# AdaLN linear-attention block: first scale block in two column halves, broadcast no-ops, later w_mod halves, half of wo on the ACT queue

## Chip, cores and metric

One core of a Trainium2 chip. The metric is device time of one execution in microseconds, the median of three runs. The profile is of one execution, taken by the hardware profiler; its span is a little shorter than the measured time.

## What is computed

Inputs are x (2048 x 1024), the projection weights wqkv and wo, the feed-forward weights w_gate, w_up and w_down, a condition c (1 x 1024) and w_mod (1024 x 6144), all bf16.

```python
mod = silu(c) @ w_mod                  # six rows of 1024: sa, ca, ga, sb, cb, gb
h = layernorm(x) * (1 + ca) + sa
q, k, v = split(h @ wqkv)              # 32 heads of 32
pq, pk = phi(q), phi(k)                # phi(t) = t+1 if t>0 else exp(t), plus 1e-6
kv = sum over tokens of pk * v ; z = sum of pk
x = x + ga * ((pq @ kv) / (pq . z + 1e-6)) @ wo
h = layernorm(x) * (1 + cb) + sb
x = x + gb * ((silu(h @ w_gate) * (h @ w_up)) @ w_down)
```

## The kernel before

Tokens are worked in four blocks of 512 (`sc` = 0 to 3), each in four tiles of 128 (`t`). A block of k or v is eight groups (`k_groups`: tile t and column half nb), each of eight matmuls over the contraction chunks cc, 128x512 outputs in one PSUM bank. Four such banks (pool `pa`, `acc_a`) rotate; four more are in pool `pb` (`acc_b`). A group's bank is free again when ACT has copied it (v, line 309) or when ACT's exp (line 273) and two DVE instructions (lines 274 and 276) have turned it into phi.

**Head.** Before block 0 can start, the scale row ca is needed: silu(c) times 1024 columns of w_mod. `wca` is loaded in eight row chunks of 1024 columns, then `wv` in eight, then `wsa` and `wk`, all on the SP queue but for the first chunk. For each chunk j, `mod_rows` multiplies it into rows in PSUM (four 32-row pieces), and one matmul with one output column makes the first scale column ahead of the others (`first`). `mod_turn` turns the rows into columns. The block is normalised, transposed on TensorE (`pe_transpose_tile`), copied to `hT`, and scaled into `hs` (`scale_to`); V of block 0 runs on `hs`. The rows of sa come later. `keep_warm` issues matmuls on a zeroed tile `sel`, whose results nobody reads. `sc_row`, silu(c) in all 128 partitions, comes from eight matmuls and two ACT copies.

**Blocks.** For sc > 0: K groups 0 and 1, then kv of the block before (`kv_phase`), K groups 2 to 7, V; then statistics and transposes (`ln1`) of the next block, laid into the same stretch. `mod_load` loads 1024 columns of w_mod transposed, as two tiles; `mod_step` is one DVE instruction (line 396) that multiplies a tile's 128x1024 rows by `sc_row` and sums them into one column. The steps are spread over K and V (`K_STEPS`, `V_STEPS`); those in V wait for a flag `one` that POOL writes behind the statistics' work. `hold_back` writes one element of a new tile, so that its load does not start before a given point. At sc = 2, `wo` is loaded in eight pieces on the SP queue; later its rows are multiplied by ga.

**Fold.** While q of blocks 1 and 2 runs, kv is multiplied into wo: `fold_wo(h, nb)` runs 16 matmuls of 32 rows by 32 columns, four row groups g by four column groups i, into four banks, and copies them back into `wo` (line 611). It is called four times, each time between q groups.

**What sets the order.** Each engine runs its instructions in the order in which they stand. In the head that order is the one written (`in_order`). Elsewhere a scheduler lays out the instructions of DVE, ACT and POOL by dependencies and its own estimates; matmuls stay in the order of the text. Buffers come from rotating pools; `k8` has 19 large tiles.

Of the kernel before, what the change touches and what calls it, by code (L numbers as in the profile page):

```python
# [21 lines left out]
def kernel(  # L22
# [13 lines left out]
    nc = tc.nc  # L36
# [77 lines left out]
    c_sb = const.tile([DC, P], BF16, name="c_sb")  # L114

# [8 lines left out]
    for st in range(2):  # L124
        load_x(st, nc.sync)
# [3 lines left out]
    wca = [big("wme", [4, D]) for _ in range(2)]  # L129
# [6 lines left out]
    for j in range(DC):  # L136
        load_block(wca, wm_v, j, D, nc.scalar if j == 0 else nc.sync)
    for cc in range(DC):
        load_block(wv, wqkv_v, cc, 2 * D)
        if cc in (1, 4):  # L140
            load_x(2 + cc // 4, nc.sync)
# [26 lines left out]
    sc_row = const.tile([P, D], BF16, name="sc_row")  # L168
# [11 lines left out]
    sel = const.tile([P, HPC, P], BF16, name="sel")  # L180
# [17 lines left out]
    def bn(src, mv_out):  # L198
        stats = small.tile([P, NNB, nc.vector.BN_STATS_DIM], F32, name="stats")
        for i in range(NNB):  # L200
            nc.vector.bn_stats(out=stats[:, i, :], in_=src[:, i * NB:(i + 1) * NB])  # L201
        nc.vector.bn_aggr(out=mv_out, in_=stats[:])

    def normalise(dst, src, mean, rstd):
        nc.vector.tensor_scalar(out=dst, in0=src, scalar1=mean, scalar2=rstd, op0=ALU.subtract, op1=ALU.mult)

    def normalise_act(dst, src, mv, rstd):
        nmr = small.tile([P, 1], F32, name="nmr")
        last_nmr[0] = nc.gpsimd.tensor_scalar(out=nmr[:], in0=mv[:, 0, 0:1], scalar1=rstd[:, 0:1], scalar2=-1.0,  # L209
                                op0=ALU.mult, op1=ALU.mult)  # L210
        nc.scalar.activation(out=dst, in_=src, func=ACT.Identity, bias=nmr[:], scale=rstd[:, 0:1])  # L211
# [5 lines left out]
    def pe_transpose_tile(hT, xn, t):  # L217
        tp = acc_b("tp", (DC, P), BF16)
        for cc in range(DC):
            transpose(tp[:, cc, :], xn[:, cc * P:(cc + 1) * P])  # L220
        nc.vector.tensor_copy(out=hT[:, :, t * P:(t + 1) * P], in_=tp[:])
# [3 lines left out]
    def ln1_stats(sc, t):  # L225
        x_sb = x_tiles.pop(sc * STC + t)
        mv = small.tile([P, STC, 2], F32, name="mv")
        bn(x_sb, mv[:, 0, :])
        rstd = rstd_of(mv, 1)
        return sc, t, x_sb, mv, rstd  # L230

    def ln1_norm(sc, t, x_sb, mv, rstd, dve=False):
        xn = k2.tile([P, D], BF16, name="xn", bufs=4)
        if dve:
            normalise(xn[:], x_sb[:], mv[:, 0, 0:1], rstd[:, 0:1])
        else:
            normalise_act(xn[:], x_sb[:], mv, rstd)
        if sc > 0:
            last_load[0] = nc.sync.dma_start_transpose(hTs[sc][:, :, t * P:(t + 1) * P], xn[:])
        return xn  # L240
# [14 lines left out]
    def mod_rows(q, lo, hi, first=None):  # L255
        for j in range(lo, hi):
            if first is not None:
                mm(first, lhsT=wca[j // 4][:, j % 4, 0:P], rhs=scT[:, j:j + 1], start=False, stop=j == DC - 1)
            row_matvec(mod_ps[:, q * MW:(q + 1) * MW], sc32[:, j, :], (wsa, wca)[q][j // 4][:, j % 4, :],
                       q == 0 and j == 0, j == DC - 1)  # L260
# [4 lines left out]
    def scale_to(hs, hT, cc, lo, hi):  # L265
        nc.vector.tensor_scalar(out=hs[:, cc, lo:hi], in0=hT[:, cc, lo:hi], scalar1=ca0T[:, cc:cc + 1], scalar2=None,
                                op0=ALU.mult)

# [105 lines left out]
    def mod_load(q, cols, held=False):  # L374
        ts = [big("wmt", [DC // 2, D]) for _ in range(2)]
        if held:
            hold_back(ts)
        for h, t in enumerate(ts):
            lo = q * D + h * NB
            last = nc.sync.dma_start_transpose(t[:], w_mod[:, lo:lo + NB])  # L380
            mod_steps.extend((t[:, i, :], cols[:, 4 * h + i:4 * h + i + 1]) for i in range(DC // 2))
        return last
# [71 lines left out]
    nc.vector.memset(sel[:], 0.0)  # L454

    def keep_warm(acc, n):
        for _ in range(n):
            mm(acc[:], lhsT=sel[:, 0, :], rhs=sel[:], start=True, stop=True)

    def keep_warm_f32(acc, n):  # L460
        zeros = sel[:].rearrange("p h n -> p (h n)").bitcast(F32)
        for _ in range(n):
            mm(acc[:, 0:zeros.shape[1]], lhsT=zeros[:, 0:P], rhs=zeros, start=True, stop=True)

    accs = [acc_a() for _ in range(4)]
    spare = accs[3]
    keep_warm_f32(spare, 3)
    keep_warm(spare, 1)
# [5 lines left out]
    with in_order(nc.vector, nc.scalar, nc.gpsimd):  # L474
        mod_ps = acc_b("mod_ps")
        mm(mod_ps[:, 0:DC], lhsT=c_sb[:], rhs=ident[0:DC, 0:DC], start=True, stop=True)
        for g in range(4):
            mm(mod_ps[g * DH:(g + 1) * DH, MW:2 * MW], lhsT=ident[:, 0:DH], rhs=base_t[:, 0:MW], start=True, stop=False)
        nc.scalar.activation(out=scT[:], in_=mod_ps[:, 0:DC], func=ACT.Silu)
        xn0 = ln1_norm(*ln1_stats(0, 0))  # L480
        st1 = ln1_stats(0, 1)
        nc.vector.tensor_copy(out=sc32[:], in_=scT[:].unsqueeze(2).to_broadcast([P, DC, DH]))
        xn1 = ln1_norm(*st1, dve=True)
        keep_warm_f32(spare, 1)
        for h in range(2):
            for j in range(DC // 2):
                mm(accs[h][:, j * P:(j + 1) * P], lhsT=scT[:, 4 * h + j:4 * h + j + 1].to_broadcast([P, P]), rhs=ident[:],
                   start=True, stop=True)
            nc.scalar.copy(out=sc_row[:, h * NB:(h + 1) * NB], in_=accs[h][:])
        keep_warm(spare, 3)  # L490
        first = accs[2][:, 0:1]
        mm(first, lhsT=ident[:], rhs=base_t[:, 0:1], start=True, stop=False)
        mod_rows(1, 0, 3, first)
        pe_transpose_tile(hT, xn0, 0)
        pe_transpose_tile(hT, xn1, 1)
        mod_rows(1, 3, DC, first)
        keep_warm(spare, 1)
        nc.vector.tensor_scalar(out=hs[:, 0, 0:H], in0=hT[:, 0, 0:H], scalar1=first, scalar2=None, op0=ALU.mult)
        mod_turn(DC, 2 * DC)
        for cc in range(1, 4):  # L500
            scale_to(hs, hT, cc, 0, H)
        xn2 = ln1_norm(*ln1_stats(0, 2))
        for cc in range(4, DC):
            scale_to(hs, hT, cc, 0, H)
        st3 = ln1_stats(0, 3)
        gs = k_groups[0:4]
        v_mms(hs, gs, accs, 0, 6)
        pe_transpose_tile(hT, xn2, 2)
        for cc in range(DC):
            scale_to(hs, hT, cc, H, H + P)  # L510
        xn3 = ln1_norm(*st3)
        v_mms(hs, gs, accs, 6, DC)
        gs2, accs2 = k_groups[4:6], [acc_b("acc") for _ in range(2)]
        v_mms(hs, gs2[0:1], accs2[0:1])
        v_evac(0, gs, accs)
        pe_transpose_tile(hT, xn3, 3)
        for cc in range(DC):
            scale_to(hs, hT, cc, H + P, SCW)
        v_mms(hs, gs2[1:2], accs2[1:2])
        mod_rows(0, 0, DC)  # L520
        mod_turn(0, DC)
        nc.vector.tensor_copy(out=sca[:], in_=scr[:, :, :, 0])
        v_evac(0, gs2, accs2)
        for g in k_groups[6:8]:
            acc = acc_a()
            v_mms(hs, [g], [acc])
            v_evac(0, [g], [acc])
        modulate_all(hT, ca1T, saT)
# [4 lines left out]
    for h in range(2):  # L533
        with tc.issue_after(last_load[0].ins):
            nc.sync.dma_start(out=wq[h][:], in_=wqkv_v[:, 4 * h:4 * h + 4, 0:D])
# [5 lines left out]
    for sc in range(NSC):  # L541
        if sc > 0:
            k_phase(sc, 0, 2)
            kv_phase(sc - 1)
            k_phase(sc, 2, 3)
            if sc == 1:
                mod_load(3, sbT, True)
                mod_step(1)
            k_phase(sc, 3, 4)
            if sc == 2:  # L550
                wo = [big("wo", [4, D]) for _ in range(2)]
                hold_back(wo)
                for h in range(2):
                    for g in range(4):
                        with tc.issue_after(last_load[0].ins):
                            last_load[0] = nc.sync.dma_start(out=wo[h][g * DH:(g + 1) * DH, :, :], in_=wo_v[h, g])
            if sc == 3:
                mod_load(4, cbT, True)
            k_phase(sc, 4, 8)
        if sc == 0:  # L560
            k_phase(0, 0, 8)
# [24 lines left out]
        if sc == 0:  # L586
            with tc.issue_after(last_load[0].ins):
                last_load[0] = mod_load(2, gaT)

    q_phase(1, 0, 1, 2)  # L590
    q_phase(1, 1, 2)
# [10 lines left out]
    def fold_wo(h, nb):  # L602
        ns = slice(nb * NB, (nb + 1) * NB)
        ps = [acc_b("wf") for _ in range(4)]
        for i in range(HPC):
            for g in range(4):
                rs = slice(g * DH, (g + 1) * DH)
                mm(ps[g][i * DH:(i + 1) * DH, :], lhsT=KVT[rs, h, i * DH:(i + 1) * DH], rhs=wo[h][rs, i, ns],
                   start=True, stop=True)
        for g in range(4):  # L610
            (nc.scalar.copy if g % 2 == 0 else nc.vector.tensor_copy)(out=wo[h][:, g, ns], in_=ps[g][:])

    q_phase(1, 2, 5)
# [5 lines left out]
    den_sum(0, acc_a())  # L619
    fold_wo(0, 0)  # L620
    den_spread(0)
    q_phase(1, 6, 8)
    fold_wo(0, 1)
    q_phase(2, 0, 2)
    fold_wo(1, 0)
    q_phase(2, 2, 4)
    fold_wo(1, 1)
# [3 lines left out]
    def wo_tile(st):  # L631
# [10 lines left out]
        for nb in range(NNB):  # L642
            ns = slice(nb * NB, (nb + 1) * NB)
            a_ps = acc_b("a_ps")
            for hg in range(HG):
                mm(a_ps[:], lhsT=pq[:, hg, t * P:(t + 1) * P], rhs=wo[hg // 4][:, hg % 4, ns],
# [145 lines left out]
```

## Time and profile before

| | |
|---|---|
| Measured time, median of 3 | 830.9 us (830.61 to 830.96) |
| Profiled span | 828.4 us |
| DVE, ACT, POOL busy | 42%, 20%, 8% of the span |
| DMA, mean rate over the span | 156 GB/s |
| DMA, mean rate over the first 30 us | 359 GB/s |

How to read it: a row of the timeline has the start and the length in us, the engine, the source line, the operation, what is written and read, the shapes, and how many instructions are merged in the row. All matmuls stand at line 98, so they are told apart by their tiles: `acc<-wv,hs` is V of block 0, `acc<-wv,hT` V of a later block, `acc<-wk,hT` is K, `kvp` is kv, `wf` the fold, `acc<-hT,wq` is q. A 128x512 matmul is shown with 379 ns, but in a stream one starts every 0.216 us, since matmuls overlap; start times are what counts. About one matmul record in fifty is missing, which looks like a gap of one matmul. In the slices of the page (40 of 20.7 us each) DMA moves most in the first two:

```profile
DMA  9968444139995836456342262753405529610011
GB/s 347 301 167 187 124 112 102 41 96 320 368 246 196 251 110 181 150 168 195 103 158 96 62 222 88 254 187 110 145 0 182 149 65 358 217 47 1 19 58 51
```

### The profile page before, as it was taken

How to read it: one execution, taken by the hardware profiler on the slowest of the kernel's cores; microseconds unless marked ns; L12 is line 12 of the kernel's file. 1: busy time of each engine (PE TensorE's matmuls, PEld its weight loads, DVE VectorE, ACT ScalarE, POOL GpSimd, SP SyncE). 2: the span in 40 equal slices, each digit the busy share in tenths (PEclk: the TensorE clock that was granted, in tenths of full speed). 3: DMA queues.
4: the chain of work that ended last, by engine and by line, in shares of the span. 5: the costliest groups of instructions: out<-in, count | busy, mean ns of one | idle time of the engine just before them, and what ended most of it. 6: DMA issues, size and time to landing. Idle time of an engine off the chain costs nothing.

```text
span 828.4 us, 11209 instructions
## 1 busy us (share of the span) xinstructions
PE 818.2 (99%) x4531; PEld 379.1 (46%) x4609; DVE 348.7 (42%) x680; ACT 168.1 (20%) x253; POOL 64.0 (8%) x165
## 2 busy tenths in 40 slices
PE   8999999999999999999999999999999999999998
PEld 4444444444444444444444444444444444444444
DVE  6868778886353344422222354222224432222222
ACT  3535343434111101101111010111111101111000
POOL 2101020120222002000000010000001100000000
PEclk9999999999999999999999999999999999999999
DMA  9968444139995836456342262753405529610011
GB/s 347 301 167 187 124 112 102 41 96 320 368 246 196 251 110 181 150 168 195 103 158 96 62 222 88 254 187 110 145 0 182 149 65 358 217 47 1 19 58 51
DMA packets 142212, 129.07 MB, mean 156 GB/s; under 512 B 58768, under 2 KB 120720, under 8 KB 141648
## 3 DMA queue, kind: packets, MB, share of 16 engines
q1 hardware_dynamic: 138208, 115.10, 46.3%
q0 software_dynamic: 3792, 12.98, 5.0%
q8 instruction: 36, 0.59, 0.3%
q10 hardware_dynamic: 160, 0.26, 0.1%
q14 instruction: 16, 0.13, 0.0%
HBM read 101.98 MB, written 12.72 MB: 138 GB/s over the span
## 4 chain that ended last, share of the span: by engine, by line
PE 97%; DMA 2%; issue 1%; DVE 0%; ACTq 0%; SPq 0%
PE acc L98 89%; PE a_ps L98 7%; DMA wv<-in_A_wqkv_dram 1%; PE kvp L98 1%; DMA wme<-in_w_mod_dram 0%; PE wf L98 0%; PE den L98 0%; PE mod_ps L98 0%; PE vb L98 0%; ACTq L126 0%; PE tp L101 0%; SPq L134 0%; DVE e L708 0%; DVE ob L711 0%
## 5 line engine op out<-in xcount | busy, mean ns | idle before, releaser
L98 PE MATMUL acc<-h2T,wgu 128*128 128x512 bf16 x1755 | 385.6, 379 | 1.9
L98 PEld LDWEIGHTS <-wgu 128*128 128x128 bf16 x1792 | 175.3, 98 | 211.3
L687 DVE TENSOR_TENSOR gu<-acc,e 128x512 bf16<-128x512 f32 x112 | 77.5, 692 | 289.9 <-PE acc L98 278.8
L98 PE MATMUL acc<-wd,gu 128*128 128x512 bf16 (+2 forms) x908 | 195.2, 372 | 0.9
L686 ACT ACTIVATE e<-acc 128x512 f32<-128x512 f32 x112 | 66.9, 597 | 374.8 <-PE acc L98 363.4
L98 PEld LDWEIGHTS <-gu 128*128 128x128 bf16 x924 | 89.3, 98 | 104.5
L708 DVE TENSOR_TENSOR e<-acc,gb_bc 128x512 f32<-128x512 f32 (+2 forms) x33 | 22.3, 675 | 131.7 <-PE acc L98 122.8
L98 PEld LDWEIGHTS <-hT 128*128 128x128 bf16 x448 | 43.6, 98 | 52.3
L98 PE MATMUL a_ps<-wo,pq 128*128 128x512 bf16 x250 | 56.9, 379 | 0.3
L98 PE MATMUL acc<-hT,wq 128*128 128x512 bf16 x250 | 55.9, 379 | 0.6 <-issue 0.5
L98 PE MATMUL acc<-wk,hT 128*128 128x512 bf16 x252 | 55.9, 379 | 0.4 <-issue 0.3
L273 ACT ACTIVATE eb<-acc 128x512 bf16<-128x512 f32 x64 | 37.6, 594 | 61.7 <-PE acc L98 57.3
L211 ACT ACTIVATE xn<-x,nmr,rstd 128x1024 bf16<-128x1024 f32 x16 | 19.8, 1240 | 126.2 <-POOL nmr L209 125.4
L98 PE MATMUL acc<-wv,hT 128*128 128x512 bf16 x186 | 41.6, 379 | 0.3
L98 PEld LDWEIGHTS <-pq 128*128 128x128 bf16 x256 | 25.1, 98 | 30.2
L655 POOL DMA_DIRECT2D x_scratch<-x x16 | 9.8, 615 | 373.5 <-DVE x L648 373.4
L98 PEld LDWEIGHTS <-wq 128*128 128x128 bf16 x256 | 24.6, 98 | 29.9 <-issue 1.1
L274 DVE TENSOR_SCALAR eb<-eb 128x512 bf16<-128x512 bf16 x64 | 18.3, 290 | 26.0 <-ACT eb L273 26.0
L648 DVE TENSOR_TENSOR x<-a_ps,x_sb 128x512 f32<-128x512 f32 x32 | 22.1, 691 | 8.6 <-PE a_ps L98 7.9
L195 POOL TENSOR_TENSOR rstd<-veps,neg_half 128x1 f32<-128x1 f32 x32 | 18.0, 561 | 99.5 <-DVE veps L193 87.0
L201 DVE BATCH_NORM_STATS2 stats<-x_sb 128x6 f32<-128x512 bf16 x32 | 20.9, 674 | 4.4 <-DMA x_sb<-in_A_x_dram 4.3
L711 DVE TENSOR_TENSOR ob<-e,x1r 128x512 bf16<-128x512 f32 (+2 forms) x33 | 22.3, 675 | 1.0
(99 smaller groups left out, 320.6 us busy)
## 6 DMA issues: line engine op xcount, KB each, us to landing
wgu<-in_B_w_gate_dram SPq DMA_DIRECT2D x28, 1024.0 KB, 6.4
wgu<-in_B_w_up_dram SPq DMA_DIRECT2D x28, 1024.0 KB, 7.9
x_sb<-in_A_x_dram SPq DMA_DIRECT2D x32, 256.0 KB, 5.3
x_scratch<-x POOLq DMA_DIRECT2D x16, 512.0 KB, 3.1
x1r<-x_scratch SPq DMA_DIRECT2D x31, 256.0 KB, 2.9
wd<-in_B_w_down_dram SPq DMA_DIRECT2D x7, 1024.0 KB, 6.7
rbc<-rden_scratch POOLq DMA_DIRECT2D x16, 256.0 KB, 8.1
out_dram<-ob SPq DMA_DIRECT2D x31, 128.0 KB, 1.7
```

The costliest lines, as they stand in the source:

```text
L98: return tc.keep_in_program_order(nc.tensor.matmul(out, lhsT=lhsT, rhs=rhs, start=start, stop=stop))
L195: nc.gpsimd.tensor_tensor(out=rstd[:, 0:n], in0=veps[:, 0:n], in1=neg_half[:].to_broadcast([P, n]), op=ALU.pow)
L201: nc.vector.bn_stats(out=stats[:, i, :], in_=src[:, i * NB:(i + 1) * NB])
L211: nc.scalar.activation(out=dst, in_=src, func=ACT.Identity, bias=nmr[:], scale=rstd[:, 0:1])
L273: nc.scalar.activation(out=e[:], in_=acc, func=ACT.Exp)
L274: nc.vector.tensor_scalar(out=e[:], in0=e[:], scalar1=1.0, scalar2=PHI_EPS, op0=ALU.min, op1=ALU.add)
L648: nc.vector.tensor_tensor(out=x1[:, ns], in0=a_ps[:], in1=x_t[:, ns], op=ALU.add)
L655: nc.gpsimd.dma_start(out=x1_dram[st * P:(st + 1) * P, :], in_=x1[:])
L686: nc.scalar.activation(out=sg[:], in_=ps[0][:], func=ACT.Silu)
L687: gm = nc.vector.tensor_tensor(out=guT[sc][f // GPT][:, f % GPT, :], in0=ps[1][:], in1=sg[:], op=ALU.mult)
L708: nc.vector.tensor_tensor(out=yt, in0=y_ps, in1=gb_bc[:, ns], op=ALU.mult)
L711: nc.vector.tensor_tensor(out=ob, in0=yt, in1=x1r, op=ALU.add)
```

## The change

It has four parts.

- **Head in two column halves.** Only the first 512 columns of ca are loaded at first, in four pieces of two row chunks, and made into four scale columns directly, by matmuls with one output column (`ca_cols`); V of block 0 starts with the contraction chunks 0 to 3, of which two row tiles stand already transposed in PSUM and are scaled from there. The other 512 columns follow behind half of wv, as rows (`ca_rows`). Six instead of four V groups run on the first half. K of block 0 takes its first two groups as a pair. This is meant to start V with less loaded.
- **No-ops from a broadcast column.** `keep_warm` uses the one-column constant `neg_half`, broadcast, instead of the zeroed tile, which goes; some no-ops are shorter and placed elsewhere. `sc_row` is now computed on one partition and spread through DRAM.
- **Later loads.** The transposed loads of w_mod come as halves, each about half a block later. kv of the block before comes after one K group instead of two. Two of the four pieces of each half of `wo` are loaded on the ACT queue.
- **Fold in three.** The fold's 16 units (h, nb, g), each four matmuls, go in lots of 5, 6 and 5 instead of four lots of 4, over banks of both pools, and are copied into new tiles `wof`.

```diff
-    for j in range(DC):
-        load_block(wca, wm_v, j, D, nc.scalar if j == 0 else nc.sync)
-    for cc in range(DC):
+    load_ca(0, nc.scalar)
+    nc.scalar.dma_start(out=sc_row[0:1, :], in_=c)
+    for cc in range(4):
         load_block(wv, wqkv_v, cc, 2 * D)
-        if cc in (1, 4):
-            load_x(2 + cc // 4, nc.sync)
+    load_ca(1, nc.sync)
+    load_x(3, nc.sync)
+    for cc in range(4, DC):
+        load_block(wv, wqkv_v, cc, 2 * D)
...
+    def keep_warm(*widths):
+        for n in widths:
+            mm(accs[3][:, 0:n], lhsT=neg_half[:].to_broadcast([P, P]), rhs=neg_half[:].to_broadcast([P, n]), start=True, stop=True)
...
+        def ca_cols(k):
+            for i in range(4):
+                for j in (2 * k, 2 * k + 1):
+                    mm(cols[i], lhsT=wca[0][:, j, i * P:(i + 1) * P], rhs=scT[:, j:j + 1], start=False,
+                       stop=j == DC - 1 and i in (0, 3))
...
+        v_mms(hs, gs, accs, 0, 1)
+        turn_half(xn1, 1, 1)
...
+        v_mms(hs, gs, accs, 3, 4)
+        ca_rows()
+        mod_turn(DC + 4, 2 * DC)
...
+        v_mms(hs, gs2, accs2, 0, 4)
...
+        v_mms(hs, gs, accs, 4, DC)
+        v_evac(0, gs, accs)
+        v_mms(hs, gs2[0:1], accs2[0:1], 4, DC)
...
+        v_mms(hs, gs3[0:1], accs3[0:1])
+        mod_rows(lambda j: wsa[j // 4][:, j % 4, :], 0, DC)
...
+    nc.gpsimd.dma_start(out=sc_dram[:], in_=sc_row[0:1, :])
+    with tc.issue_after(wq_load.ins):
+        nc.sync.dma_start(out=sc_row[:], in_=sc_dram[:].to_broadcast([P, D]))
...
-            k_phase(sc, 0, 2)
+            k_phase(sc, 0, 1)
             kv_phase(sc - 1)
-            k_phase(sc, 2, 3)
+            k_phase(sc, 1, 3)
             if sc == 1:
-                mod_load(3, sbT, True)
+                mod_load(2, gaT, (1,), True)
+                mod_load(3, sbT, (0,), True)
                 mod_step(1)
             k_phase(sc, 3, 4)
             if sc == 2:
+                last_load[0] = mod_load(3, sbT, (1,), True)
                 wo = [big("wo", [4, D]) for _ in range(2)]
                 hold_back(wo)
+                behind = last_load[0].ins
                 for h in range(2):
-                    for g in range(4):
-                        with tc.issue_after(last_load[0].ins):
+                    for g in range(2):
+                        nc.scalar.dma_start(out=wo[h][(2 + g) * DH:(3 + g) * DH, :, :], in_=wo_v[h, 2 + g])
+                        with tc.issue_after(behind):
                             last_load[0] = nc.sync.dma_start(out=wo[h][g * DH:(g + 1) * DH, :, :], in_=wo_v[h, g])
...
-                last_load[0] = mod_load(2, gaT)
+                last_load[0] = mod_load(2, gaT, (0,))
...
+    wof = [big("wof", [4, D]) for _ in range(2)]
+    fold_units = [(h, nb, g) for h in range(2) for nb in range(NNB) for g in range(4)]
+
+    def fold_wo(accs):
+        units = [(fold_units.pop(0), acc) for acc in accs]
         for i in range(HPC):
-            for g in range(4):
+            for (h, nb, g), acc in units:
                 rs = slice(g * DH, (g + 1) * DH)
-                mm(ps[g][i * DH:(i + 1) * DH, :], lhsT=KVT[rs, h, i * DH:(i + 1) * DH], rhs=wo[h][rs, i, ns],
-                   start=True, stop=True)
+                mm(acc[i * DH:(i + 1) * DH, :], lhsT=KVT[rs, h, i * DH:(i + 1) * DH],
+                   rhs=wo[h][rs, i, nb * NB:(nb + 1) * NB], start=True, stop=True)
...
-    den_sum(0, acc_a())
-    fold_wo(0, 0)
+    den_sum(0)
+    fold_wo([acc_b("wf") for _ in range(3)] + [acc_a() for _ in range(2)])
     den_spread(0)
     q_phase(1, 6, 8)
-    fold_wo(0, 1)
-    q_phase(2, 0, 2)
-    fold_wo(1, 0)
-    q_phase(2, 2, 4)
-    fold_wo(1, 1)
+    q_phase(2, 0, 1)
+    fold_wo([acc_b("wf") for _ in range(4)] + [acc_a() for _ in range(2)])
+    q_phase(2, 1, 4)
+    fold_wo([acc_b("wf") for _ in range(4)] + [acc_a()])
```

## The prediction

> **What bounds the kernel now.** I read the page's shares first, then the chain of waits, then three stages of the timeline. The page:
>
> ```profile
> PE 818.2 (99%) x4531; PEld 379.1 (46%) x4609; DVE 348.7 (42%) x680; ACT 168.1 (20%) x253; POOL 64.0 (8%) x165
> PE 97%; DMA 2%; issue 1%; DVE 0%; ACTq 0%; SPq 0%
> ```
>
> TensorE is busy for 818.2 of 828.4 us, and 97% of the chain that ended last is PE. So only what shortens or stretches PE's own sequence counts. The table of PE's waits holds 1.2, 0.8, 0.7 and 0.5 us, and all but part of the 0.8 us of issue lies ahead of 12 us. The chain over the first 30 us shows what the head waits for:
>
> ```profile
> 5.52 5.48 DMA wv<-in_A_wqkv_dram
> ...
> 11.02 6.37 DMA wv<-in_A_wqkv_dram
> ...
> 17.43 3.61 PE acc L98 x16
> ```
>
> The first V matmul waits for the wv block that lands at 11.00, then for one at 17.39; from there PE runs without a break, and K starts at 27.60 (timeline). The head is bound by arrivals, the rest by PE. The stage that decides my forecast is not the head but the end of K in block 2 (sc=2), on DVE:
>
> ```profile
> 95.81 0.67 DVE L276 SCALAR_TENSOR_TENSOR pk<-acc,eb 128x512 bf16<-128x512 f32 x1
> 96.40 1.21 DVE L396 SCALAR_TENSOR_TENSOR wmt<-wmt,sc_row 128x1024 bf16<-128x1024 bf16 x1
> ...
> 98.42 0.67 DVE L276 SCALAR_TENSOR_TENSOR pk<-acc,eb 128x512 bf16<-128x512 f32 x1
> ...
> 99.87 0.67 DVE L276 SCALAR_TENSOR_TENSOR pk<-acc,eb 128x512 bf16<-128x512 f32 x1
> ...
> 103.09 0.67 DVE L276 SCALAR_TENSOR_TENSOR pk<-acc,eb 128x512 bf16<-128x512 f32 x1
> ...
> 104.71 0.15 DVE L193 TENSOR_SCALAR veps<-mv 128x1 f32<-128x1 f32 x1
> ...
> 106.03 1.28 DVE L396 SCALAR_TENSOR_TENSOR wmt<-wmt,one,sc_row 128x1024 bf16<-128x1024 bf16 x1 [0.83 <-POOL one L391]
> ```
>
> The four pk lines are the evacuations of K groups 4, 5, 6 and 7. Each frees one of the four PSUM banks of pool pa. They stand between the LayerNorm statistics of the next block, and all of them come ahead of the four modulation steps that start at 106.03.
>
> **What the Trainium skill says.** (1) "TensorE: Matmul & The Clock Gate", section "Architectural detail": matmuls keep program order and ACT and DVE are strict FIFO. The trace agrees: every DVE row above starts at or after the one before it, so an instruction put ahead delays all behind it. (2) Same page, Part 1: about 3.4 us of idleness halves the PE clock, and about 3.4 us of sustained work brings it back. No PE gap after 12 us is long enough to test the first half here; at the start, 128-column transposes run 16 in 1.07 us at 8.02, 0.056 us apart, which is the page's warm figure. (3) Same page, Part 3: matmuls on different 32x32 tiles of the array overlap. The trace agrees: 16 fold matmuls take 0.43 us. (4) "DMA: Bandwidth & Descriptors", "Issuing engines are not separate DMA queues": a second issuing queue saves only sequencer time. So half of wo on the ACT queue gains nothing in itself.
>
> **The change part by part.**
>
> Head. Transfers of 256 KB land 0.67 us apart when the queue is full (8 wk issues, each released by a landing, take 5.05 us from 18.57: (5.05-0.33)/7). Before, wv's first block is the 11th block (2 x, 8 wme), at 11.00. After, it is the 8th (3 x, 4 wme half-pieces), near 9.0. Their rows are 1 KB instead of 2 KB; on the page 1 MB of wgu (1 KB rows) lands in 6.4 us and 1 MB of wd (2 KB rows) in 6.7, so I charge nothing. Column sums, scale and rows then go on: V starts near 9.5 instead of 11.13. The next limit is the second half of the scale columns, the 15th block, at 11.00+4x0.67 = 13.7; its last rows take 0.2. From 13.9 PE still has 48 V matmuls at 0.216 (16 take 3.61-0.16, the last one's tail), 8 transposes (0.45) and the 32 rows of saT (1.06 at 23.15): 10.4+0.45+1.06 gives 25.8 for the start of K, against 27.60. A floor: the last wk block lands near 28.7 (last issue 23.29, 5.4 to landing), and the new pair of K groups needs it for its last two matmuls, so it ends at 29.2 at the earliest, against 31.05. I take -1.5 us: 1.8 less 0.3 for short waits on xn3 and on the first K evacuation. Bounds -1.9 and 0.
> The no-op matmuls from neg_half, the sc_row round trip through DRAM (needed first near 61 us, loaded behind wq near 37) and the half-tile copies on ACT cost nothing: they lie in PE's wait for DMA or in ACT's 80% idle time.
>
> Later w_mod halves and K/kv order. The steps are as many as before (1, 4, 3, 4, 4, 6, 2); each half lands at least one stage ahead of its first step. kv one K group earlier moves 128 matmuls and adds none: 0.
>
> Fold of wo. Before, four folds of 16 matmuls:
>
> ```profile
> 158.32 0.81 PE L98 MATMUL acc<-hT,wq 128*128 128x512 bf16 x3
> 159.06 0.43 PE L98 MATMUL wf<-wo,kvs 32*32 32x512 bf16 x16
> 159.43 0.82 PE L98 MATMUL acc<-hT,wq 128*128 128x512 bf16 x3
> ```
>
> The third q matmul starts at 158.32+2x0.216 = 158.75, so from the last q matmul to the next one, at 159.43, is 0.67 us; less the 0.216 that q streams anyway, a fold costs 0.45, four cost 1.82. All 16 use different tiles of the array. After, there are three folds of 5, 6 and 5 units; the fifth unit repeats a row group, so its matmul meets a tile still in use and, in FIFO order, holds up all that follow. Repeats on the same tiles do serialise: 32 saT rows of 256 columns on four tiles take 1.06 us, 8 rounds of 0.11. So a fold takes 5 streams of 0.216 in place of one: 0.45+4x0.216 = 1.31, three cost 3.94. That is +2.1 us; bounds -0.45 (one fold less, all overlapping) and +2.1.
>
> DVE order in block 2. The new order of instructions, in the changed kernel's line numbers, is:
>
> ```
> L287 pk<-acc  (K group 4)      <- V group 0 waits for this
> L407 step; the other 6 statistics, 4 aggregates, 4 veps
> L416, L418                     ga turned
> L407 x4 steps, waiting for `one` (POOL)
> L285, L287 pk<-acc (K group 5) <- V group 1 waits for this
> L285 x2, L287 x2   (K groups 6, 7)
> ```
>
> The ACT order is five exponentials, the four wo transfers, three exponentials. The banks rotate, so V group 1's first matmul waits for K group 5's evacuation, now behind the four steps. With before's durations: as before until 97.54; then the statistics without the three evacuations. These took 3x0.8, and 0.34 of idleness goes too, so the last veps ends near 102.1 instead of 104.86. `one` came 1.2 later (106.03), so the steps start at 103.3; four of 1.2 end at 108.1; the evacuation (0.2+0.69 and a gap) ends at 109.1. V starts at 99.18, so PE wants V group 1 at 99.18+1.73 = 100.9. **PE stands still for 8.2 us**, which nothing hides, since PE is the bound. The steps' durations are measured, so the bounds are narrow: 7.5 and 8.8. The stall is over twice the skill's 3.4 us, so V resumes at half clock. Cold for 3.4 us costs 1.7, for 6.8 us 3.4; a window in which half the work is enough would cost 0.8. I take 2.1.
>
> Sum: 830.9-1.5+2.1+8.2+2.1 = **841.8 us**.
>
> **Rivals.**
> A, the stall does not come, since the evacuations are reached early or V finds another bank: head and fold remain, 830.9-1.5+2.1 = 831.5. For it: PE never waits for DVE there now. Against: the order is fixed in the program and DVE is serial.
> B, faster: as A, and the fifth fold unit overlaps, 830.9-1.5-0.45 = 829.0. For it: three folds have fewer transitions than four. Against: the 8 rounds of the saT rows.
> C, the stall and nothing gained: the narrow matmuls do not keep the clock up, V's first part runs cold and the head's gain is gone, and the clock takes its full 6.8 us after the stall: 830.9+0+2.1+8.2+3.4 = 844.6.
>
> **How the numbers follow.** Main case 0.78, A 0.08, B 0.06, C 0.08. The main case spans, with its terms' ends not all at once, 838.5 to 843.5; the range goes up to C and down to 838.5, and A and B (0.14) are left out. Faster by over 0.2% is B: 0.06; within 0.2% is A: 0.08; slower 0.86.
>
> **What would show it.** Right: PE gap of about 8 us after the first eight V matmuls of block 2, ended by DVE pk L287; V matmuls after it 0.43 apart for some us; 20, 24 and 20 fold matmuls over 1.1 us each; K starting near 26. Wrong: no PE wait for DVE near 100 us, folds of 0.4 us, or V no earlier than 11.

## The result, and the profile after

| | before | after |
|---|---|---|
| Measured time, median of 4 executions each | 830.75 us | 840.6 us |
| Ratio, 95% interval | | 1.0121, 1.0106 to 1.0137 |
| Profiled span | 828.4 us | 839.7 us |
| V of block 2, first matmul to K of block 3 | 13.8 us | 24.8 us |

The change makes the kernel 1.2% slower. The page of the kernel after, busy time and granted TensorE clock:

```profile
PE 825.9 (98%) x4629; PEld 381.0 (45%) x4629; DVE 346.0 (41%) x684; ACT 174.0 (21%) x261; POOL 65.1 (8%) x167
PEclk9999979999999999999999999999999999999999
```

The busy times of the two pages can't be set against each other directly: the page before lacks some matmul records (4531 matmuls beside 4609 weight loads), this one lacks none. What stands out is one slice of 21 us (the sixth, from 105 us) with a granted clock under 0.8. The longest of PE's waits in the kernel after (total, times, longest, in us; all others are under 1 us):

```profile
PE acc L98 <- DVE pk L287: 8.4, 1, 8.4
```

It is a wait for an evacuation (line 287), which the kernel before did not have. The timeline of DVE in that stretch, K group 4's evacuation first:

```profile
96.09 0.67 DVE L287 SCALAR_TENSOR_TENSOR pk<-acc,eb 128x512 bf16<-128x512 f32 x1
...
102.09 0.15 DVE L200 TENSOR_SCALAR veps<-mv 128x1 f32<-128x1 f32 x1
...
103.86 1.28 DVE L407 SCALAR_TENSOR_TENSOR wmt<-wmt,one,sc_row 128x1024 bf16<-128x1024 bf16 x1 [1.26 <-POOL one L402]
...
107.48 1.28 DVE L407 SCALAR_TENSOR_TENSOR wmt<-wmt,one,sc_row 128x1024 bf16<-128x1024 bf16 x1
...
109.01 0.69 DVE L287 SCALAR_TENSOR_TENSOR pk<-acc,eb 128x512 bf16<-128x512 f32 x1
109.62 0.48 DVE L285 TENSOR_SCALAR eb<-eb 128x512 bf16<-128x512 bf16 x2
110.02 1.28 DVE L287 SCALAR_TENSOR_TENSOR pk<-acc,eb 128x512 bf16<-128x512 f32 x2
```

Between the evacuations of groups 4 and 5 lie 12.9 us: statistics until 102.2, then four steps, of which the first waits for `one`. PE in the kernel before:

```profile
99.18 13.98 PE L98 MATMUL acc<-wv,hT 128*128 128x512 bf16 x62
113.00 3.62 PE L98 MATMUL acc<-wk,hT 128*128 128x512 bf16 x16
```

and in the kernel after:

```profile
99.46 1.89 PE L98 MATMUL acc<-wv,hT 128*128 128x512 bf16 x8
109.76 14.63 PE L98 MATMUL acc<-wv,hT 128*128 128x512 bf16 x56 [8.41 <-DVE pk L287]
124.23 1.89 PE L98 MATMUL acc<-wk,hT 128*128 128x512 bf16 x8
```

Eight matmuls, the stall, and then 56 matmuls that take until 124.23, 14.5 us instead of 56 x 0.216 = 12.1. The clock by stretches (start:end, length, busy time of PE, PEld, DVE, ACT, POOL, then PEclk, DMA share and GB/s):

```profile
104.00:108.00 4.00, 0.00 (x0) 0.00 (x0) 4.00 (x7) 2.50 (x3) 1.87 (x4) 0.55 1.10 181
108.00:112.00 4.00, 2.24 (x6) 0.86 (x6) 3.27 (x8) 0.00 (x0) 0.00 (x0) 0.50 1.07 200
112.00:116.00 4.00, 4.00 (x14) 1.50 (x12) 0.00 (x0) 0.79 (x2) 0.58 (x1) 0.67 1.22 287
```

The clock halves during the stall and stays so for about 4.9 us of work, until some 114.6 (worked out from the clock of 0.67 between 112 and 116); that costs 2.4 us.

### The profile page after: what moved, and what is told of

It is laid out like the page before. It is cut to its first block, busy times and chain, and to the rows that moved or that the text cites. A ratio compares the mean times of both kernels' runs of the same rounds, so it can differ in the third digit from the quotient of the medians.

```text
span 839.7 us, 11345 instructions
## 1 busy us (share of the span) xinstructions
PE 825.9 (98%) x4629; PEld 381.0 (45%) x4629; DVE 346.0 (41%) x684; ACT 174.0 (21%) x261; POOL 65.1 (8%) x167
## 3 DMA queue, kind: packets, MB, share of 16 engines
HBM read 102.24 MB, written 12.72 MB: 137 GB/s over the span
## 4 chain that ended last, share of the span: by engine, by line
PE 96%; DVE 2%; DMA 1%; SPq 0%; issue 0%; POOL 0%; ACT 0%; ACTq 0%; POOLq 0%
PE acc L98 88%; PE a_ps L98 7%; DMA wme<-in_w_mod_dram 1%; DVE wmt L407 1%; PE kvp L98 1%; DVE stats L208 0%; DVE pk L287 0%; PE den L98 0%; SPq L141 0%; PE mod_ps L98 0%; SPq L136 0%; PE wf L98 0%; DVE eb L285 0%; PE vb L98 0%; ACT eb L284 0%
## 5 line engine op out<-in xcount | busy, mean ns | idle before, releaser
L98 PE MATMUL a_ps<-wof,pq 128*128 128x512 bf16 x256 | 57.4, 379 | 0.0
L98 PE MATMUL acc<-wv,hT 128*128 128x512 bf16 x192 | 44.5, 394 | 8.4 <-DVE pk L287 8.4
L320 ACT CAST v<-acc 128x512 bf16<-128x512 f32 x32 | 18.1, 586 | 29.9 <-PE acc L98 29.9
```

The costliest lines, as they stand in the source:

```text
L98: return tc.keep_in_program_order(nc.tensor.matmul(out, lhsT=lhsT, rhs=rhs, start=start, stop=stop))
L320: nc.scalar.copy(out=vs[sc][:, t * D + nb * NB:t * D + (nb + 1) * NB], in_=acc[:])
```

## The experiments

Each kernel's times stand beside the kernel before on the same chip (829.95 to 830.06 us there). The points used below, in us from the span's start, all first matmuls read from the timelines of PE:

| kernel | V block 0 | K block 0 | V block 2 | K block 3 |
|---|---|---|---|---|
| before | 11.13 | 27.60 | 99.18 | 113.00 |
| after | 9.36 | 27.32 | 99.46 | 124.23 |
| 1, all of wo on SP | 10.67 | 27.37 | 99.57 | 116.93 |
| 2, before + wo on ACT | 11.18 | 27.61 | 99.19 | 124.23 |
| 3, before + 1 KB rows | 11.49 | 27.54 | 99.15 | 112.96 |
| 4, no-ops in the stall | 8.99 | 25.87 | 98.18 | 120.56 |
| 5, steps behind evacuations | 11.08 | 27.78 | 99.79 | 121.89 |
| 6, and statistics between | 9.62 | 26.91 | 99.65 | 122.39 |
| 8, new head only | 9.39 | 26.30 | 98.02 | 111.83 |
| 9, loads and wo as before | 9.22 | 26.37 | 98.86 | 112.67 |
| 12, wo on ACT, orders mended | 9.50 | 26.40 | 98.35 | 112.16 |

**1. All of wo back on the SP queue.**

```diff
-                    for g in range(2):
-                        nc.scalar.dma_start(out=wo[h][(2 + g) * DH:(3 + g) * DH, :, :], in_=wo_v[h, 2 + g])
-                        with tc.issue_after(behind):
+                    for g in range(4):
+                        with tc.issue_after(last_load[0].ins):
```

> The changed kernel with all eight pieces of wo back on the SP queue; all else as changed. Theory 1 (the ACT queue half of wo is what put the evacuations of K groups 5 to 7 behind four modulation steps in DVE order): no wait of PE for DVE pk in V of block 2, no half clock near 105 us: 840.6 - 8.4 - 2.2 = 830.0 us, V of block 2 as in the changed kernel, at 99.5. Theory 2 (the later w_mod halves, with their held tiles, are the cause): stall of about 8 us stays, 840.6. The prediction's head and fold terms (-1.5 and +2.1) would give 831.5 here; the trace of the changed kernel says that both were mis-sized (+0.3 and +0.2), which gives 831.3 to 831.4 without the stall if the half clock cost 1.2 only, 830.0 if it cost 2.4.

835.24 us, ratio 1.0068 (1.0055 to 1.0081). The wait for pk is gone, as theory 1 said, but 5 us of the loss are not. The waits of PE show another one:

```profile
PE acc L98 <- DVE hT L223: 3.4, 1, 3.4
```

The timeline of the SP queue in the kernel before:

```profile
94.66 3.65 SPq L556 DMA_DIRECT2D wo<-in_A_wo_dram  x8
101.72 7.08 SPq L239 DMA_TRANSPOSE hT<-xn  x4
```

and in this one:

```profile
94.94 4.08 SPq L391 DMA_TRANSPOSE wmt<-in_w_mod_dram  x1
99.20 3.76 SPq L607 DMA_DIRECT2D wo<-in_A_wo_dram  x8
103.07 10.18 SPq L246 DMA_TRANSPOSE hT<-xn  x4
```

Before, the four transposes of the next block's hT took from 101.72 to 108.8. Now a transposed half of w_mod stands ahead of wo, wo is issued 4.5 us later, and the transposes behind it last until 113.3. The last lands at 116.3, and K of block 3 waits for it. After this wait the clock is at 0.50 from 116 to 122 us, so the wait of 3.4 us is not the whole cost: K of block 3 takes 17.6 us until V, against 15.1 in experiment 9. Neither theory had this: the later w_mod loads have a cost of their own. How it comes about is only in part the issue order: the transposes begin 1.4 us later, but the four take 10.2 us in place of 7.1 and land 8.6 us after their issue in place of 3.4 (medians). Whether the load's place in the queue or the bytes that it moves beside them does the most here, no run separates.

**2. Half of wo on the ACT queue, in the kernel before.** The reverse of that diff, and nothing else of the change.

> The kernel before with one edit: half of the wo pieces on the ACT queue. Theory 1 (this edit alone moves the evacuations in DVE order): PE waits 8 to 8.5 us for DVE pk after the first eight V matmuls of block 2 and runs at half clock after it, 830.8 + 8.4 + 2.2 = 841.4. Theory 2 (it needs the later w_mod halves too): no stall, 830.8.

840.84 us, ratio 1.0130 (1.0115 to 1.0146): theory 1. The timeline of PE is that of the kernel after, to a few tenths:

```profile
99.19 1.89 PE L98 MATMUL acc<-wv,hT 128*128 128x512 bf16 x8
109.47 14.92 PE L98 MATMUL acc<-wv,hT 128*128 128x512 bf16 x56 [8.39 <-DVE pk L276]
```

This one edit, which moves no work to or from DVE, makes the whole stall: the four steps stand ahead of the evacuations of groups 5 to 7 here too, and group 5's starts at 108.73. Why the scheduler then lays DVE's instructions out differently was not looked into.

**3. Short rows.** The kernel after receives its second half of ca late in its profile (PE still waits for it at 15.06, where the prediction had 13.7), and its w_mod pieces have 1 KB rows. So the kernel before was given such rows.

```diff
-    for j in range(DC):
-        load_block(wca, wm_v, j, D, nc.scalar if j == 0 else nc.sync)
+    for k in range(4):
+        for h in range(2):
+            js = slice(2 * (k % 2), 2 * (k % 2) + 2)
+            (nc.scalar if k + h == 0 else nc.sync).dma_start(
+                out=wca[k // 2][:, js, h * NB:(h + 1) * NB],
+                in_=wm_v[:, 2 * k:2 * k + 2, D + h * NB:D + (h + 1) * NB])
```

> The kernel before with the eight first w_mod blocks loaded as pieces of 2 row chunks by 512 columns (1 KB rows) instead of 1 chunk by 1024 columns (2 KB rows): same bytes, same place in the queue. Theory 1 (1 KB rows move slower, some 300 instead of 390 GB/s, and this ate the gain of the new head): 2.1 MB take 7.0 instead of 5.4 us, V of block 0 starts near 12.7 instead of 11.1, total 832.4. Theory 2 (row length costs nothing, the late arrivals have another cause): V near 11.1, 830.8.

830.06 us, ratio 1.0003 (0.9994 to 1.0011). V of block 0 starts 0.36 later and K of block 0 no later. Theory 1, which had V at 12.7 and 832.4 us, is out: row length is not what ate the head's gain.

**4. No-ops in the stall.**

```diff
             acc = acc_a()
+            if sc == 2 and g == k_groups[1]:
+                noop = acc_b("noop")
+                for _ in range(36):
+                    mm(noop[:], lhsT=ident[:], rhs=wv[0][:, 0, 0:NB], start=True, stop=True)
             v_mms(hTs[sc], [g], [acc])
```

> The changed kernel with 36 matmuls that nobody reads (128x512, 36 x 0.216 = 7.8 us) put on TensorE between V groups 0 and 1 of block 2, that is into the stall. Theory 1 (stall and half clock are two separate costs; PE idleness is what lowers the clock): the stall ends as before near 109.7, but the clock stays at 1.0, so the V matmuls after it are 0.216 apart: 840.6 - 2.4 = 838.2 us. Theory 2 (the slow matmuls after the stall have another cause, or the clock falls for another reason): 840.6.

839.15 us, ratio 1.0114 (1.0100 to 1.0128). The total lies between the theories, since the head starts at another time in each execution; the stretch itself decides. Timeline of PE:

```profile
98.18 1.89 PE L98 MATMUL acc<-wv,hT 128*128 128x512 bf16 x8
99.91 7.93 PE L98 MATMUL noop<-wv,ident 128*128 128x512 bf16 x36
108.48 12.25 PE L98 MATMUL acc<-wv,hT 128*128 128x512 bf16 x56 [0.63 <-DVE pk L287]
120.56 2.15 PE L98 MATMUL acc<-wk,hT 128*128 128x512 bf16 x8
```

The stall still ends with the evacuation, but the 56 matmuls now take 12.1 us, and from V of block 2 to K of block 3 it is 22.38 us instead of 24.77. The mean clock is 1.000 in all four executions, against 0.994 to 0.996 in the kernel after. Theory 1: stall and half clock are two costs, 8.4 and 2.4 us, and it is TensorE's idleness that lowers the clock.

**5 and 6. The DVE order mended.** First the four steps behind the last evacuation (5), then also the statistics of tile t behind that of K group 4+t (6); wo stays on ACT and the w_mod loads stay late.

```diff
-        mod_step(V_STEPS[sc], scaled.ins if sc == NSC - 1 else last_veps[0].ins, sc + 1 < NSC)
+        with tc.issue_after(last_phi[0].ins):
+            mod_step(V_STEPS[sc], scaled.ins if sc == NSC - 1 else last_veps[0].ins, sc + 1 < NSC)
...
-            ln1(sc + 1, [last_on[nc.vector.engine]] * 2 + [i.ins for i in last_phi[2:4]] if sc == 0 else [last_phi[-5].ins] * STC)
+            ln1(sc + 1, [last_on[nc.vector.engine]] * 2 + [i.ins for i in last_phi[2:4]] if sc == 0 else [i.ins for i in last_phi[-4:]])
```

> The changed kernel with wo still half on the ACT queue, and one edit: the four modulation steps are queued behind the evacuation of K group 7 on DVE. Theory 1 (the stall is purely DVE order): the evacuation of group 5 now comes right after the statistics and two small ga instructions, which end near 102.6 on the changed kernel's clock, so it is done near 103.6 and PE waits 2.4 us instead of 8.4, too short for the half clock: 840.6 - 6.0 - 2.4 = 832.2 us, less or more by the 1.5 us that the head varies. And the transposes of the next block's hT stay early enough (half of wo is off the SP queue), so K of block 3 waits for nothing, unlike the version with all of wo on SP. Theory 2 (the ACT issues themselves delay the exponentials, so the evacuations would be late in any order): stall of 6 us or more, 838 or more.

> As the version with the steps behind the evacuations, and the statistics of token tile t of the next block are queued behind the evacuation of K group 4+t, so that groups 5 to 7 are evacuated while they run, as in the kernel before. Theory 1: no wait of PE for DVE in V of block 2, none for hT in K of block 3: 840.6 - 8.4 - 2.4 = 829.8 us, with the head's spread 828.5 to 831; against 830.1 before the change. Theory 2 (something else of the change costs as well): a wait of over 1 us remains in blocks 1 to 3.

841.37 us (ratio 1.0134, 1.0121 to 1.0148) and 842.47 us (1.0153, 1.0139 to 1.0167): nothing is won, against the first theory of both; for (6) the second came true, that something else of the change costs as well. The stall itself did what theory 1 said, 2.2 us in (5) and none in (6), so the ACT issues do not hold the evacuations up by themselves. But the waits of PE in (5) are

```profile
PE acc L98 <- DVE hT L223: 5.8, 1, 5.8
PE acc L98 <- DVE pk L287: 2.2, 1, 2.2
```

and in (6) the wait for hT is 8.8 us. The SP queue in (5):

```profile
95.17 8.36 SPq L391 DMA_TRANSPOSE wmt<-in_w_mod_dram  x1
103.70 5.63 SPq L608 DMA_DIRECT2D wo<-in_A_wo_dram  x4
109.44 1.23 SPq L246 DMA_TRANSPOSE hT<-xn  x1
```

The transposed half of w_mod holds the queue for 8.4 us here, against 4.1 us in (1), where no wo transfers on the ACT queue run beside it. And the waits of the SP queue show a wo issue behind it that waited 3.9 us for that load to land:

```profile
SPq L608 <- DMA wmt<-in_w_mod_dram: 3.9, 1, 3.9
```

Here the order in the queue does hold the transposes up. The first transpose of hT goes out at 109.4, 7.7 us later than in the kernel before. In the kernel after it is the same, issued at 108.29, but PE's longer stall for DVE hides it: its last modulated hT is ready near 121.6, and K of block 3 comes at 124.23.

**7. The fold on busy tiles**, on top of (6). The units are sorted by row group, so that up to four matmuls in a row use the same 32x32 tile.

```diff
-    fold_units = [(h, nb, g) for h in range(2) for nb in range(NNB) for g in range(4)]
+    fold_units = [(h, nb, g) for g in range(4) for h in range(2) for nb in range(NNB)]
```

> As the version with the statistics between the evacuations, with the units of the wo fold in another order: the 16 units sorted by row group, so that in each lot four or five of the matmuls that follow each other use the same 32x32 tile (lots of 5, 6, 5: row groups 00001, 111222, 23333). Theory 1 (each tile has a queue of its own; a matmul on a free tile goes ahead of one that waits): a lot lasts as long as its busiest tile, 4, 3 and 4 streams of 0.216, about 1.0, 0.8 and 1.0 us from the first fold matmul to the next q matmul instead of 0.59 each; together +1.1 us. Theory 2 (matmuls start strictly in program order, as the prediction had it): 13 or more streams in the lots with four of a row group, 2.8 us and more each; together over +5 us.

The whole is 841.49 us (1.0136, 1.0121 to 1.0152), with the wait for hT of (6) in it, so the fold is read from the timeline. Its last two lots (the rows between are the second lot's) in (7):

```profile
173.05 0.60 PE L98 MATMUL wf<-wo,kvs 32*32 32x512 bf16 x9
...
173.87 5.35 PE L98 MATMUL acc<-hT,wq 128*128 128x512 bf16 x23
179.16 0.87 PE L98 MATMUL wf<-wo,kvs 32*32 32x512 bf16 x16
179.82 0.42 PE L98 MATMUL acc<-wo,kvs 32*32 32x512 bf16 x4
180.18 5.14 PE L98 MATMUL acc<-hT,wq 128*128 128x512 bf16 x22
```

From the first fold matmul to the next q it is 0.82 and 1.02 us (and 1.02 in the first lot), as three and four streams of 0.216 on the busiest tile give. Strict order would take 13 streams in the lots with four of a row group. So theory 1's times; that each tile keeps a queue of its own is one picture that fits them. The same in the kernel after, second and third lot:

```profile
172.25 0.45 PE L98 MATMUL wf<-wo,kvs 32*32 32x512 bf16 x16
172.47 0.44 PE L98 MATMUL acc<-wo,kvs 32*32 32x512 bf16 x8
172.84 5.35 PE L98 MATMUL acc<-hT,wq 128*128 128x512 bf16 x24
178.12 0.44 PE L98 MATMUL wf<-wo,kvs 32*32 32x512 bf16 x16
178.35 0.42 PE L98 MATMUL acc<-wo,kvs 32*32 32x512 bf16 x4
178.71 1.47 PE L98 MATMUL acc<-hT,wq 128*128 128x512 bf16 x6
```

From the first fold matmul to the next q, each lot takes 0.59 us, as two streams give; all 16 `wf` matmuls start together although some `acc` ones, which repeat a tile and start 0.22 later, stand ahead of them in the program.

**8. The new head alone.** The changed kernel up to K of block 0, and from there on everything as before the change.

```diff
-            k_phase(sc, 0, 1)
+            k_phase(sc, 0, 2)
             kv_phase(sc - 1)
-            k_phase(sc, 1, 3)
+            k_phase(sc, 2, 3)
...
-                mod_load(2, gaT, (1,), True)
-                mod_load(3, sbT, (0,), True)
+                mod_load(3, sbT, held=True)
...
-    fold_wo([acc_b("wf") for _ in range(3)] + [acc_a() for _ in range(2)])
+    fold_wo(0, 0)
```

> The new head alone (column halves, broadcast no-ops, paired first K groups, sc_row through DRAM) with everything from block 1 on as before the change: loads of w_mod and wo, kv after two K groups, four folds. Theory 1 (the head gains up to 1.7 us when arrivals and clock play along, about nothing when the first w_mod piece lands a microsecond late or the clock window falls badly): runs spread over 826.5 to 830.5 span-free times of 828.3 to 831, median 829.5 against 830.1, wider spread than before. Theory 2 (the prediction's head term): 828.6 in nearly all runs. Theory 3 (head costs): 830.5 or more.

829.26 us against 830.02, ratio 0.9994 (0.9985 to 1.0002); 13 executions from 828.72 to 831.74, those of the kernel before from 829.48 to 830.91. Theory 1. This is the fastest version that was run, but its interval reaches past 1.

**9. Both load edits undone.** The changed kernel with w_mod loaded where it was (below) and all of wo on SP (the diff of 1).

```diff
-                mod_load(2, gaT, (1,), True)
-                mod_load(3, sbT, (0,), True)
+                mod_load(3, sbT, held=True)
...
-                last_load[0] = mod_load(3, sbT, (1,), True)
...
-                last_load[0] = mod_load(2, gaT, (0,))
+                last_load[0] = mod_load(2, gaT)
```

> The changed kernel with both load edits undone: w_mod loaded where it was before, all of wo on the SP queue; new head, kv after one K group and the three-lot fold stay. Theory 1 (the whole loss comes from the stretch V of block 2 to K of block 3, from these two edits together): no wait of PE for DVE pk or hT there, 829.3 of the new head alone + 0.3 (kv one K group earlier, 15.40 instead of 15.07 us from K to V of block 1) + 0.2 (three lots of the fold instead of four) = 829.8 us. Theory 2 (some of the loss lies elsewhere): 831 or more.

829.75 us, ratio 0.9997 (0.9989 to 1.0005): theory 1. With (1), (2) and the kernel after this makes four corners: neither load edit 829.75; later w_mod loads alone 835.24; wo on ACT alone, run on the kernel before and not on the changed one, 840.84; both 840.6. The costs do not add: (5) and (6) showed that the two waits lie on top of each other.

**10 to 12. Is the ACT queue itself at fault?** All three keep half of wo on ACT, with the w_mod loads as before. (10) has the DVE order of (6). (11) has the statistics one K group earlier (`last_phi[-5:-1]`). (12) is (11) with

```diff
         if sc == 0:
-            nc.sync.dma_start(out=x_t[:], in_=x2[st * P:(st + 1) * P, :])
+            with tc.issue_after(last_load[0].ins):
+                nc.sync.dma_start(out=x_t[:], in_=x2[st * P:(st + 1) * P, :])
```

> As the version with the statistics between the evacuations, half of wo still on the ACT queue, and the w_mod loads where they were before. Theory 1 (the later half of w_mod, put ahead of wo and of the next block's transposes on the SP queue, is what makes hT late): with it gone, K of block 3 follows V of block 2 without a wait, and since the DVE order is mended too, 829.8 us. Theory 2 (wo on the ACT queue delays the transposes by itself): a wait for hT of 2 us or more ahead of K of block 3 remains, 832 or more.

> As the version with the w_mod loads where they were before and half of wo on the ACT queue, with one difference in DVE order: the statistics of tiles 0 and 1 come ahead of the evacuations of K groups 5 to 7, those of tiles 2 and 3 behind them, so that the last statistics end near 104.7 as in the kernel before, instead of 104.9 on a clock that began 0.8 us earlier. Theory 1 (the remaining wait of 3.3 us for hT came from the late statistics of tiles 1 to 3, an effect of that experiment's own order; the ACT queue costs nothing by itself): wait for hT under 0.5 us, 829.8 us. Theory 2 (half of wo on the ACT queue delays the transposes by itself, by crowding the transfers): a wait for hT of 1.5 to 3.3 us remains, 832 to 834.

> As the last version (half of wo on the ACT queue, w_mod loads where they were, statistics and evacuations mixed), with the three x loads of the later wo stage queued on SP behind the four hT transposes of block 3, as they are in the kernel before, instead of between them. Theory 1 (the remaining wait of 1.5 us for hT is again a matter of order, here on the SP queue; the ACT queue costs nothing by itself): no wait for hT, 832.3 - 1.5 - some 0.8 for the slower start of K of block 3 = 830.0 us. Theory 2 (transfers of wo issued on two queues crowd the transposes): the wait stays at 1 us or more, 831.5 or more.

834.26 us (1.0050, 1.0037 to 1.0064), 832.30 us (1.0032, 1.0020 to 1.0044) and 829.67 us (0.9995, 0.9987 to 1.0003). (10) and (11) missed their first theory: waits for hT of 3.3 and 1.5 us remained, as the second theory of each had it, that the ACT queue itself delays the transposes. (12) then spoke against it. Earlier statistics, the only edit from (10) to (11), took 1.8 us off it. The SP queue in (11) shows x loads of a later stage between the transposes:

```profile
101.70 1.26 SPq L246 DMA_TRANSPOSE hT<-xn  x1
103.06 0.51 SPq L691 DMA_DIRECT2D x_sb<-in_A_x_dram  x1
103.67 1.24 SPq L246 DMA_TRANSPOSE hT<-xn  x1
105.00 0.52 SPq L691 DMA_DIRECT2D x_sb<-in_A_x_dram  x1
```

and in (12):

```profile
93.73 1.75 SPq L606 DMA_DIRECT2D wo<-in_A_wo_dram  x4
102.03 6.56 SPq L246 DMA_TRANSPOSE hT<-xn  x4
108.64 3.34 SPq L692 DMA_DIRECT2D x_sb<-in_A_x_dram  x4
```

where K of block 3 follows V of block 2 after 13.81 us, as before the change. So, with the w_mod loads where they were, half of wo on the ACT queue costs nothing once DVE and SP have orders like the old ones. It brings nothing either: (12) and (9) agree within their intervals.

## Why the prediction was right, and which steps were not

The forecast of 841.8 us has its main step right in place, size and cause. It is the only large term that shows in the total: with experiment 2, one edit of the four, the loss is there whole.

- **DVE order, +8.2.** Measured 8.4. The last veps ends at 102.24 (forecast 102.1), steps from 103.86 (103.3), evacuation done at 109.7 (109.1).
- **Half clock, +2.1.** Measured 2.4 in the profiled execution, by experiment 4. The 2.1 was the middle of 0.8 and 3.4, so that it came this close is in part luck: in experiment 2 two executions took 841.5 us at a mean clock of 0.993 and two 840.2 at 0.996, so this cost differs by some 1.3 us between executions.
- **Head, -1.5.** Right sign, too large: experiment 8 gives -0.76 at the median, and its interval reaches past no gain at all. V of block 0 starts at 9.0 to 9.6 in eight of the eleven profiles with the new head (forecast 9.5), and K at 25.9 to 26.4 in six of them, against the 25.8 worked out; in the other five K comes at 26.9 to 29.0. The length of V's last part was right: in experiments 1, 4 and 8 alike it takes 11.9 us to K, as forecast. What varies is when that part can begin: at 14.0 in experiment 4 (forecast 13.9), at 15.3 in the kernel after. The term's own sum stopped at K of block 0: from there to q, the kernel of experiment 8 spends 13.93 us against 13.81. And the head's gain is easily lost. In the profile after, the first w_mod piece landed at 6.32, in experiment 4 at 4.97, with K at 27.32 and 25.87. Row length costs 0.36 us at V and nothing in the total (experiment 3), so the prediction could leave it out, though of the page's two wgu lines it used only that with 6.4 us; the other has 7.9. What makes a piece late in one execution stays open.
- **Fold, +2.1.** Here the mechanism failed. The prediction said that a matmul that meets a busy tile "holds up all that follow", five streams a lot, citing the Trainium skill ("TensorE: Matmul & The Clock Gate") for the order; the page states it in Part 3, section "The mechanism", where matmuls start and end strictly in program order. Experiment 7 shows otherwise: only the same tile waits. Page and measurement differ, and the measurement decides; for these matmuls the sentence on order ahead of the prediction doesn't hold either. The fold's term measures +0.2 in place of +2.1 (from q of block 1 to the first wgu matmul it is 59.94 us before and 60.13 after). The 32 rows of saT that it argued from fit this too: on four tiles only, 8 rounds are the busiest tile's own.
- **kv one K group earlier, 0.** Measured +0.3 in the kernel after: from K to V of block 1, 15.40 us instead of 15.07, with a short wait at kv. In the nine experiments that keep this edit the same stretch takes 15.07 to 16.10, so the size is not firm.
- **Later w_mod halves, 0.** Wrong, though the total doesn't show it. "Lands ahead of its first step" was the wrong question for these loads; what stands behind them on the SP queue is the next block's hT. Alone they cost about 5.5 us (experiment 1 against 9). In the kernel after they are hidden behind the larger stall, and take its place when that is mended (5, 6).

With the measured sizes the sum is 830.75 - 0.8 + 0.2 + 0.3 + 8.4 + 2.4 = 841.3 in place of 841.8, against 840.6: the head and the fold were off in opposite directions, so the total's closeness is in part luck too. One reading was off without effect: of the waits that the prediction lays ahead of 12 us, 0.3 us of that for wv falls at 17.4.

## What to carry to other kernels

Moving a DMA issue to another engine's queue is an edit to the schedule: read the new order of every engine's instructions around it, and look for an evacuation that now stands behind a long wait. Before mending a stall, ask which wait would end next: here a second one of about the same length lay under it, and only undoing both edits (9), or undoing one and mending the orders of DVE and SP for the other (12), brought the time back. A load's cost is not only when it lands but what stands behind it in its queue.

## What the hardware showed beyond this

Matmuls on 32x32 tiles did not start in program order: those on free tiles went ahead by 0.22 us of one whose tile was busy, and a lot lasted as long as its busiest tile.

The clock halved in the PE waits of 3.3 us and more (3.3 in experiment 10, 3.4 in 1, 5.8 in 5, 7.5 in 7, 8.4 in 2 and the kernel after, 8.8 in 6), and stayed at 1.00 through those of 2.2 us (5) and 1.5 us (11).

In three of the eleven profiles with the new head (experiments 1, 5 and 7) a later row of no-op matmuls, from 6.25 or 6.72 us on, still ran at half pace, its four matmuls taking 1.63 us instead of 0.90; V of block 0 then starts at 10.7 to 11.1. The kernel before, whose V waits for data until 11, has room for that; the new head has not. The profiles with a late K of block 0 are these three and two whose first w_mod piece landed after 6.2 us (the kernel after and 6); in the six others that piece landed by 5.4. That is an agreement between traces; no run tested that these two make up the head's whole spread.
